# A longer pause in the preparation of w_out's sums, an earlier cast of one product's weights, and earlier last stores, in a fused attention and feed-forward kernel

## The chip, the cores and the metric

The kernel runs on one core of one Trainium2 chip. The core has a matrix engine (PE), a vector engine (DVE), a scalar engine (ACT), and queues that issue transfers; in this kernel nearly all transfers are issued by the queue SP, and some by ACT. The metric is the device time of the whole launch in microseconds, the median of the runs shown: 1046.59 us before (three runs, 1045.86 to 1046.83).

## The reference

The reference computes attention with a sigmoid in the place of softmax, puts the heads side by side, and sends the result through a feed-forward block of two products with a leaky ReLU between:

```python
# q, k, v: (8, 12, 448, 64); w_in: (768, 2048); w_out: (2048, 768)
scores = (1 / sqrt(64)) * q @ k.T - log(448)
attn = 1 / (1 + exp(-scores))
x = heads_side_by_side(attn @ v)          # (3584, 768)
h = x @ w_in
g = maximum(0.01 * h, h)
out = (g @ w_out).astype(float32)         # (3584, 768)
```

The 96 heads are worked as 48 pairs. Products keep the accuracy of float32: each operand is split into a high and a low part of a type that PE multiplies at full rate, and a product is the sum of three: high by high, high by low, low by high. "CAST" on ACT (or "COPY" on DVE) makes a high part, and a subtraction on DVE (`TENSOR_TENSOR w<-wx,w`, `lo<-x,hi` and so on) the low part.

## The kernel before

**Three stages.** In the first (0 to about 254 us of the span) 24 rounds work two head pairs each: scores (`sc`), sigmoid on ACT (`s<-sc`), and the product with v (`pv`). In the second (to about 661 us) x is multiplied with w_in in four groups of rows p, and for each group in four units u; a unit is a Strassen-like scheme of seven products n in the order 0, 1, 4, 5, 3, 6, 2, each of two halves of 18 matmuls, about 1.8 us a half. Their sums in PSUM (`px_h`, `py_h`, `pz_h`) are copied by ACT and added by DVE to four results (`c_h`), which ACT takes through the leaky ReLU; DVE forms further sums of them (`s`), and all are stored to memory (`g_n`). In the third stage 52 products of 36 matmuls each, 7.2 us, multiply sums of the stored g (a product's operand `gf` is a sum of up to three loaded tiles `g`, its parts are `gh` or a reused `g1s`, and `g`) with sums of w_out (`w_k`), in two accumulators in turn (`acc_A`, `acc_B`), from which DVE and ACT read outputs (`o`).

**The weights are prepared meanwhile.** The weights come as 64-bit numbers and are turned into float32 and summed by DVE, in work that fills gaps: the generator `prep()` (line 385) does it in small steps, first for the 8 units of w_in and then for the 8 units of w_out. A unit of w_out is read in four pieces of five conversions each (`wd<-wr`, `wd<-wd`); after the second piece 4 blocks, after the third 2 blocks are stored, and after the fourth `second()` (line 354) works through the table STEPS: sums among the eight blocks of two tiles `d` and `s`, with stores of blocks that are done (`t<-wd`, to the memory that the third stage loads as `w<-t`). In the middle, right after the store of `d` blocks 6 and 7, the table has an entry `("wait",)`; there the generator yields some steps with no work, as `rest()` (line 350) says. The fourth sum behind the pause, "s7" below, overwrites block 7 of `s`, and the store that reads `s` blocks 5 to 7 is issued after a unit's first sum; a sum that overwrites a stored block must wait until that store has landed. `d` and `s` change roles from unit to unit.

**What sets the order.** Every instruction is held in program order on its engine. `slot()` (line 169) counts `now`; `later(n, f)` puts f into the slot n ahead. A round of attention has five slots, a half product of the second stage one, a product of the third stage one. In attention `prepare(pace, time)` gives `prep()` a number of steps a slot; in the second stage `fill()` gives up to four steps a slot as long as a modelled DVE queue is short. `now` is 123 when the second stage begins. Before the change `rest()` yields 9 steps when `now` is below ALONE = 100 and 1 step afterwards.

**Last stores.** `after()` (around line 713) takes each finished result: leaky ReLU one slot later, store two or three slots later. For the last unit of the last group (`ends`) the stores go through ACT's queue, in ACT's order, the others through SP's.

**The first products of the third stage.** `work()` (line 1059) orders what stands at product k: low parts, reads of the accumulator, `whole()` and `high()` of operands up to k + 3, `high()` and `low()` of weights. `weights[WW[0]]` is `w_3`, the weights of the fourth product (k = 3): the first three are loaded and split during the second stage. `g_load(k)` (line 982) loads the operands up to k + FAR as far as tiles are spare; tiles are handed out from a list, so which tile an operand's sum gets depends on what was loaded before it. A transfer also waits for the one eight before it on the same hardware lane.

Of the kernel before, what the change touches and what calls it, by code (L numbers as in the profile page):

```python
# [26 lines left out]
AHEAD, FAR, SPARE = 5, 6, 1  # L27
GG, OO, WW = 7, 8, (3, 3)
# [2 lines left out]
PACES = 4, 5, 4.2, 2.8, 2  # L31
TIMES = 1.92, 1.92, 2.33, 2.33, 1.66
PRODUCT, LESS, MOST = 1.8, 0.2, 4
WAIT, REST = 9, 1
ALONE = 100
LATER = 4
IDLE = 7
# [60 lines left out]
def attn_ffn_kernel(ctx: ExitStack, tc: tile.TileContext, qk, v, w_in, w_out, out):  # L98
# [60 lines left out]
    def leaky(out, in_):  # L159
        act(out=out, in_=in_, func=AF.Prelu, alpha=0.01)  # L160


    now, chores = 0, {}

    def later(slots, *fns, first=False):

        chores.setdefault(now + slots, ([], []))[not first].extend(fns)

    def slot(work=None):
        nonlocal now  # L170
        for fns in chores.pop(now, ()):
            for fn in fns:
                fn()
        if work is not None:
            work()
        now += 1
# [52 lines left out]
    class Quad:  # L229
# [14 lines left out]
        def take(self, what, acc, how=copy):  # L244
            t = self.pool.tile([P, 2, S], F32, tag=self.tag, name=f"{what}_{self.name}", bufs=self.bufs)
            how(out=t, in_=acc)
            return t
# [101 lines left out]

    def rest():  # L350

        return (None for _ in range(WAIT if now < ALONE else REST))

    def second(u, k, dec):

# [28 lines left out]
    def prep():  # L384
# [22 lines left out]
        for at, (m, k) in enumerate(pieces):  # L407
# [29 lines left out]
            if k == n - 1:  # L437
                prepared.add((w, u))
                if w == 0:
                    yield from rest()  # L440
# [139 lines left out]
    class Operands:  # L580
# [30 lines left out]
        def sum(self, n, a, b):  # L611
            if n == 2 and self.s2 is None:
                self.s2 = take(f"s2_{self.p}", F32)
            to, fn, x, y = {
                3: (self.x(0), sub, self.x(0), self.x(2)),
                2: (self.s2, sub, self.x(3), self.x(0)),
                1: (self.x(2), add, self.x(2), self.x(3)),
                4: (self.x(1), sub, self.x(1), self.s2)}[n]
            fn(to[:, a:b], x[:, a:b], y[:, a:b])
            if b == NB:  # L620
                self.got.add(n)
# [62 lines left out]
    class First:  # L684
# [26 lines left out]
        def after(self, quad, c, u, n):  # L711
            got = quad.done(n)
            if got is None:
                return
            p = self.p
            row, col, t = got

            ends = p == NQ - 1 and u == NU // 2 - 1

            def save(x, t):  # L720
                (dma_act if ends else dma)(out=gd[p][x][:, 2 * u % KQ:2 * u % KQ + 2], in_=t)

            def name(row, col):
                return f"{((0, 3), (1, 2))[2 * u // KQ][col]}{row}"

            def made(x, fn, a, b):
                new = st.tile([P, 2, S], F32, tag="st", name=f"{x}_{p}_{u}", bufs=ST)
                (add if fn == "add" else sub)(new, c[a], c[b])
                c[x] = new
                later(2, lambda: save(x, new))  # L730

            c[name(row, col)] = t
            if n != 2:
                later(1, lambda: leaky(t, t))
            later(2 if n == 2 else 3, lambda: save(name(row, col), t))
            z = LATER if u == NU // 2 - 1 and p < NQ - 1 else 0
            have = set(c)
            i = 0
            for x in MADE[p % 2]:
                if x[0] not in c.planned and {x[2], x[3]} <= have | c.planned:  # L740
                    c.planned.add(x[0])
                    later(2 + i + z, lambda x=x: made(*x))
                    i += 1
# [22 lines left out]
    def go(todo, work):  # L766


        for x, what in todo:
            for y in what.split():  # L770
                later(0, lambda x=x, y=y: x.do(y))
        slot(work)
# [77 lines left out]
    total = NF * NQ // 2  # L850
    spare, homes = [(gp, f"g{n}") for n in range(GG)], {}
# [125 lines left out]
    operands = []  # L977
    for k in range(total):
        operands.append(Operand(k))
    ahead = 0  # L980

    def g_load(k):

        nonlocal ahead
        room = SPARE + sum(x.needs() for x in operands[:k + 5] if x.x is None)
        while ahead < min(k + FAR + 1, total) and len(spare) >= len(operands[ahead].new) - len(operands[ahead].raw) + room:
            operands[ahead].load()
            ahead += 1

    weights = [Wide(k, t2a) for k in range(WW[0])]  # L990
# [4 lines left out]
    ahead = READY + 2  # L995
# [27 lines left out]
    ends = max(i for i, x in enumerate(PRODUCTS) if x[2] and x[1] == PRODUCTS[-1][1])  # L1023
    outs, accs = {}, {}

    def place(p, o):
        c, pair, t = (int(x) for x in o)
        b = 4 * p + 2 * pair + t
        return out[NM * c:NM * c + NM, :, b * S:(b + 1) * S]

    def store(p, o):
        dma(out=place(p, o).rearrange("m p s -> p m s"), in_=outs.pop((p, o)))
# [8 lines left out]
    def read(k):  # L1041
        p, i = divmod(k, NF)
        for x in PRODUCTS[i][4]:
            how, o = x[0], x[1:4]
            if how == "c":
                outs[p, o] = outp.tile([P, NM, S], F32, tag="out", name=f"o{p}_{o}")
            for rows, acc in accs[PRODUCTS[i][1]][1]:
                take(how, outs[p, o][:, rows], acc)
            if x[4:]:
                later(1, lambda o=o: store(p, o))  # L1050

    g_load(-1)
    for x in weights[WW[0]:AHEAD]:
        x.load()
    for k in range(total):
        p, i = divmod(k, NF)
        _, lane, begins, _, reads = PRODUCTS[i]
        ending = k == total - 1
        def work():
            for x in operands[k:k + 3]:  # L1060
                if x.hi and not x.has_low:
                    x.low()
            if k:
                read(k - 1)
            for x in operands[k:k + 4]:
                if x.x is None:
                    x.whole()
                    x.high()
            for x in weights[WW[0]:k + 4]:
                if k and not x.has_high:  # L1070
                    x.high()
                elif x.has_high and not x.has_low and x.k < k + 3:
                    x.low()
            if begins:
                if p == NQ // 2 - 1 and i == ends:
                    three = [psum(x, f"acc_{x}{k}") for x in ("one0", "one1", lane)]
                    three[2] = three[2][:, 0]
                    accs[lane] = [x[:, :S] for x in three], [(slice(m, m + 1), x[:, None, :S]) for m, x in enumerate(three)]
                else:
                    t = psum(lane, f"acc_{lane}{k}")  # L1080
                    accs[lane] = [t[:, m, :S] for m in range(3)], [(slice(0, 3), t[:, :, :S])]
            me, w = operands[k], weights[k]
            for m in range(NM):
                todo = [(e, part, n) for e in range(KQ) for part, n in ((0, 0), (0, 1), (1, 0))]
                acc = accs[lane][0][m]
                for at, (e, part, n) in enumerate(todo):
                    mm(acc, lhsT=w.of(part, e, m), rhs=(me.hi, me.lo)[n].t[:, e],
                       start=begins and at == 0, stop=at == len(todo) - 1, skip_group_check=True)
                if ending:

                    x, = reads
                    o = x[1:4]
                    t, to = outs[p, o][:, m], place(p, o)[m]
                    for cols, queue in zip(HALVES, (dma, dma_act)):
                        take(x[0], t[:, cols], acc[:, cols])
                        queue(out=to[:, cols], in_=t[:, cols])

            me.done()
            if WW[0] <= k + AHEAD < total:
                weights[k + AHEAD].load()  # L1100
            g_load(k)

        slot(work)
# [45 lines left out]
```

## Time and profile before

| | |
|---|---|
| median of three runs | 1046.59 us (1045.86 to 1046.83) |
| the profiled execution's own time | 1049.28 us |
| its span, from the first to the last instruction | 1047.2 us |
| granted clock of TensorE, mean | 0.995 |
| PE busy | 1032.3 us, 99% of the span |
| DVE busy | 844.9 us, 81% |
| ACT busy | 583.9 us, 56% |
| DMA | 286 GB/s over the span |

The profiled execution is a fourth one, 2.69 us longer than the median of the runs. In the rows of the timeline, the first number is the start in us from the span's start, the second the time until the row's last instruction ends; then the engine, the line, the operation, the tile written and those read, the shape, and how many instructions the row holds. In brackets stands the idle time of the engine before it and what ended it. All instructions have the line of one helper (L135), so they are told apart by the tiles.

### The profile page before, as it was taken

How to read it: one execution, taken by the hardware profiler on the slowest of the kernel's cores; microseconds unless marked ns; L12 is line 12 of the kernel's file. 1: busy time of each engine (PE TensorE's matmuls, PEld its weight loads, DVE VectorE, ACT ScalarE, POOL GpSimd, SP SyncE). 2: the span in 40 equal slices, each digit the busy share in tenths (PEclk: the TensorE clock that was granted, in tenths of full speed). 3: DMA queues.
4: the chain of work that ended last, by engine and by line, in shares of the span. 5: the costliest groups of instructions: out<-in, count | busy, mean ns of one | idle time of the engine just before them, and what ended most of it. 6: DMA issues, size and time to landing. Idle time of an engine off the chain costs nothing.

```text
span 1047.2 us, 15127 instructions
## 1 busy us (share of the span) xinstructions
PE 1032.3 (99%) x5738; PEld 865.6 (83%) x5738; DVE 844.9 (81%) x992; ACT 583.9 (56%) x610; POOL 0.3 (0%) x5
## 2 busy tenths in 40 slices
PE   9999999999999999999999999989999999999998
PEld 5545555545899999999999999979999999999997
DVE  4778898788998999999855657598998888899883
ACT  6778787876554655555545555464363536444430
POOL 0000000000000000000000000000000000000000
PEclk9999999999999999999999999989999999999999
DMA  7888787889889898899876878996668798766823
GB/s 274 295 281 283 268 279 257 299 292 314 272 300 356 280 346 302 315 350 376 315 238 207 302 281 319 377 360 267 255 244 306 268 402 312 270 226 247 322 94 131
DMA packets 113847, 300.62 MB, mean 287 GB/s; under 512 B 9712, under 2 KB 51824, under 8 KB 113776
## 3 DMA queue, kind: packets, MB, share of 16 engines
q1 hardware_dynamic: 111760, 295.20, 79.2%
q10 hardware_dynamic: 2016, 4.47, 1.2%
q8 instruction: 45, 0.74, 0.3%
q14 instruction: 26, 0.21, 0.1%
HBM read 202.77 MB, written 96.86 MB: 286 GB/s over the span
## 4 chain that ended last, share of the span: by engine, by line
PE 94%; DVE 3%; DMA 1%; issue 0%; ACT 0%; ACTq 0%; DVEq 0%
PE px_h L135 21%; PE acc_A L135 18%; PE acc_B L135 18%; PE pz_h L135 11%; PE pv L135 11%; PE sc L135 10%; PE py_h L135 5%; DVE wd L135 2%; DMA t<-wd 1%; PE acc_one L135 0%; DVE w L135 0%; DVE lo L135 0%; DVE qks L135 0%; DVE x L135 0%; DVE gf L135 0%
## 5 line engine op out<-in xcount | busy, mean ns | idle before, releaser
L135 PE MATMUL px_h<-hi,w 128*128 128x448 f32 x768 | 223.6, 362 | 2.0 <-DVE w L135 2.0
L135 PEld LDWEIGHTS px_h<-hi,w 128*128 128x128 f32 x768 | 143.8, 187 | 11.9 <-DVE w L135 2.4
L135 PE MATMUL acc_A<-gh,w 128*128 128x448 f32 x528 | 152.5, 363 | 0.0
L135 DVE TENSOR_TENSOR w<-wx,w 128x768 fp32r<-128x768 f32 x112 | 106.8, 953 | 48.8 <-ACT w L135 48.8
L135 PE MATMUL px_h<-lo,w 128*128 128x448 f32 x384 | 139.2, 362 | 0.0
L135 ACT ACTIVATE s<-sc 128x896 f32<-128x896 f32 x144 | 119.7, 934 | 11.7 <-PE sc L135 11.7
L135 PE MATMUL acc_B<-gh,w 128*128 128x448 f32 x416 | 122.6, 369 | 3.1 <-ACT o L135 2.0
L135 PE MATMUL pz_h<-hi,w 128*128 128x448 f32 x384 | 113.0, 362 | 1.2 <-DVE w L135 1.2
L135 PE MATMUL pv<-s,v 128*64 128x448 f32 x576 | 113.8, 544 | 0.0
L135 PEld LDWEIGHTS acc_A<-gh,w 128*128 128x128 f32 x528 | 99.1, 188 | 6.5
L135 PEld LDWEIGHTS sc<-qks 64*128 64x128 f32 x876 | 80.9, 189 | 25.7 <-issue 16.9
L135 PE MATMUL sc<-qks 64*128 64x448 f32 (+1 forms) x876 | 96.5, 371 | 2.4 <-DVE x L135 2.2
L135 ACT CAST w<-wx 128x768 fp32r<-128x768 f32 x112 | 91.3, 832 | 4.4 <-DMA wx<-t 4.4
L135 PEld LDWEIGHTS pv<-s,v 128*64 128x64 f32 x576 | 39.1, 137 | 64.0 <-issue 54.1
L135 ACT ACTIVATE c_h<-c_h 128x896 f32<-128x896 f32 x48 | 45.8, 954 | 82.2 <-DVE c_h L135 82.2
L135 DVE TENSOR_TENSOR w<-w 128x1536 fp32r<-128x1536 f32 x52 | 90.9, 1750 | 0.0
L135 PEld LDWEIGHTS acc_B<-gh,w 128*128 128x128 f32 x416 | 79.6, 192 | 9.2 <-ACT o L135 2.4
L135 PE MATMUL acc_B<-g,w 128*128 128x448 f32 x328 | 85.6, 365 | 0.0
L135 PEld LDWEIGHTS pz_h<-hi,w 128*128 128x128 f32 x384 | 71.9, 187 | 5.9 <-DVE w L135 1.5
L135 PEld LDWEIGHTS px_h<-lo,w 128*128 128x128 f32 x384 | 72.1, 188 | 5.6
L135 ACT CAST w<-w 128x1536 fp32r<-128x1536 f32 x52 | 76.6, 1476 | 0.1
L135 DVE SCALAR_TENSOR_TENSOR wd<-wr,wd 128x384 int32<-128x384 int32 x128 | 71.3, 557 | 3.4
(97 smaller groups left out, 1585.0 us busy)
## 6 DMA issues: line engine op xcount, KB each, us to landing
wx<-t SPq DMA_DIRECT2D x112, 384.0 KB, 4.8
w<-t SPq DMA_DIRECT2D x52, 768.0 KB, 4.3
g<-g SPq DMA_DIRECT2D x34, 896.0 KB, 7.0
g<-c_h SPq DMA_DIRECT2D x60, 448.0 KB, 4.5
g<-s SPq DMA_DIRECT2D x48, 448.0 KB, 5.5
qk<-in_qk SPq DMA_DIRECT2D x46, 448.0 KB, 5.3
g1s<-g SPq DMA_DIRECT2D x18, 896.0 KB, 6.6
wr<-in_w_in SPq DMA_DIRECT2D x32, 384.0 KB, 4.7
```

What stands on the lines that cost most here:

```text
L135: return lambda *args, **kw: tc.keep_in_program_order(issue(*args, **kw))
```

## The change

Four things change. First, `rest()` yields 9 steps as long as `now` is below FFN = 126, that is to the end of attention, and 3 instead of 1 afterwards. Second, the last unit's stores on ACT's queue are put one slot behind the result instead of two or three. Third, `g_load(0)` loads one operand less than before. Fourth, at k = 1 the cast of `w_3` is put ahead of operand 4's sum and cast, and its low part ahead of operand 4's low part.

```diff
-WAIT, REST = 9, 1
+WAIT, REST = 9, 3
+FFN = 126
 ALONE = 100
@@ def rest():
-        return (None for _ in range(WAIT if now < ALONE else REST))
+        return (None for _ in range(WAIT if now < FFN else REST))
@@ after()
             if n != 2:
                 later(1, lambda: leaky(t, t))
-            later(2 if n == 2 else 3, lambda: save(name(row, col), t))
+            later(1 if ends else 2 if n == 2 else 3, lambda: save(name(row, col), t))
@@ g_load(k)
-        while ahead < min(k + FAR + 1, total) and len(spare) >= len(operands[ahead].new) - len(operands[ahead].raw) + room:
+        while ahead < min(k + FAR + 1 - (k == 0), total) and len(spare) >= len(operands[ahead].new) - len(operands[ahead].raw) + room:
             operands[ahead].load()
             ahead += 1
@@ work()
             if k:
                 read(k - 1)
+            if k == 1:
+                weights[WW[0]].high()
             for x in operands[k:k + 4]:
                 if x.x is None:
                     x.whole()
                     x.high()
             for x in weights[WW[0]:k + 4]:
                 if k and not x.has_high:
                     x.high()
-                elif x.has_high and not x.has_low and x.k < k + 3:
+                elif x.has_high and not x.has_low and (x.k < k + 3 or k == 1):
                     x.low()
```

The number of instructions on each engine stays as it was, and PE's order too. On DVE the order near the end of attention (the sums of w_out's second unit, and the last rounds' splits `qks` and copies `x`) was:

```order
L135 TENSOR_TENSOR wd_1_2190<-wd_1_2190 128x192
L135 SCALAR_TENSOR_TENSOR wd_1_2190<-wd_1_2190 128x384
L135 TENSOR_TENSOR qks_2646<-qk_2496,qks_2646 128x832
L135 TENSOR_TENSOR wd_1_2190<-wd_1_2190 128x192
L135 TENSOR_TENSOR wd_0_2189<-wd_1_2190 128x192
L135 TENSOR_TENSOR wd_1_2190<-wd_1_2190 128x192
L135 TENSOR_TENSOR qks_2664<-qk_2557,qks_2664 128x832
L135 SCALAR_TENSOR_TENSOR wd_1_2190<-wd_0_2189,wd_1_2190 128x192
L135 TENSOR_TENSOR wd_0_2189<-wd_1_2190 128x192
L135 COPY x_2690<-pv_2648 128x448
```

and now it is:

```order
L136 SCALAR_TENSOR_TENSOR wd_1_2190<-wd_1_2190 128x192
L136 TENSOR_TENSOR qks_2646<-qk_2496,qks_2646 128x832
L136 TENSOR_TENSOR qks_2662<-qk_2557,qks_2662 128x832
L136 COPY x_2683<-pv_2648 128x448
L136 TENSOR_TENSOR wd_1_2190<-wd_1_2190 128x192
L136 SCALAR_TENSOR_TENSOR wd_1_2190<-wd_1_2190 128x384
L136 TENSOR_TENSOR wd_1_2190<-wd_1_2190 128x192
L136 TENSOR_TENSOR wd_0_2189<-wd_1_2190 128x192
L136 TENSOR_TENSOR wd_1_2190<-wd_1_2190 128x192
L136 SCALAR_TENSOR_TENSOR wd_1_2190<-wd_0_2189,wd_1_2190 128x192
```

The sum s7 of this unit, `wd_0_2189<-wd_1_2190 128x192` (the first row of that form), stood ahead of a `qks` and of the `COPY x`; now both `qks` and the `COPY x` stand ahead of it.

On DVE at the first products of the second stage (the low parts of its weights, `w_0_n`, beside the sums of w_out's third unit) the order was:

```order
L135 TENSOR_TENSOR wd_0_2189<-wd_0_2189 128x192
L135 TENSOR_TENSOR wd_1_2190<-wd_0_2189 128x192
L135 TENSOR_TENSOR wd_0_2189<-wd_0_2189 128x192
L135 SCALAR_TENSOR_TENSOR wd_0_2189<-wd_1_2190,wd_0_2189 128x192
L135 TENSOR_TENSOR w_0_0_2896<-wx_0_2728,w_0_0_2896 128x2x384
L135 TENSOR_TENSOR wd_1_2190<-wd_0_2189 128x192
L135 TENSOR_SCALAR wd_1_2190<-wr_3_0_2776 128x384
L135 TENSOR_TENSOR w_0_1_2910<-wx_1_2782,w_0_1_2910 128x2x384
```

and now it is:

```order
L136 TENSOR_TENSOR wd_0_2189<-wd_0_2189 128x192
L136 TENSOR_TENSOR w_0_0_2884<-wx_0_2718,w_0_0_2884 128x2x384
L136 SCALAR_TENSOR_TENSOR wd_0_2189<-wd_0_2189 128x192
L136 TENSOR_TENSOR w_0_1_2902<-wx_1_2769,w_0_1_2902 128x2x384
L136 COPY x_2801<-pv_2870 128x448
L136 TENSOR_TENSOR lo_0_2941<-x_654,hi_0_2929 128x1344
L136 TENSOR_TENSOR w_0_4_2943<-wx_4_2797,w_0_4_2943 128x2x384
L136 TENSOR_TENSOR wd_0_2189<-wd_0_2189 128x192
L136 SCALAR_TENSOR_TENSOR wd_0_2189<-wd_0_2189 128x384
L136 TENSOR_TENSOR wd_0_2189<-wd_0_2189 128x192
L136 TENSOR_TENSOR wd_1_2190<-wd_0_2189 128x192
```

The first weights' low parts stood behind the unit's s7 (`wd_1_2190<-wd_0_2189 128x192`, the first of the two rows of that form); now three of them stand ahead of it, the first with four of the unit's sums between.

On ACT at the fourth product of the third stage (casts of operand 4, of `w_3` and of `w_4`, and the copy of the accumulator `acc_B` that frees it) the order was:

```order
L135 COPY o_111_6476<-acc_A_6429 128x1344
L135 CAST g1s_4_6417<-gf_6478 128x1792
L135 CAST w_3_6421<-w_3_6421 128x1536
L135 CAST w_4_6423<-w_4_6423 128x1536
L135 COPY o_101_6526<-acc_B_6484 128x1344
```

and now it is:

```order
L136 COPY o_111_6474<-acc_A_6429 128x1344
L136 CAST w_3_6421<-w_3_6421 128x1536
L136 CAST g1s_4_6417<-gf_6477 128x1792
L136 CAST w_4_6423<-w_4_6423 128x1536
L136 COPY o_101_6527<-acc_B_6483 128x1344
```

The cast of `w_3` stands ahead of operand 4's; the copy of `acc_B` still stands behind all three. On DVE the low part of `w_3` moves likewise from behind operand 5's sum to a place right behind operand 4's sum. That sum, `gf<-g_4,g_4`, lies in another tile than before: the old one also held sums `s` of the second stage, and the sum waited for four transfers, stores of `s` among them; in the new one it waits for the two loads of its own operands.

## The prediction

> **What bounds the kernel now.** I read the page's first part, then the waits of PE, then the timelines of DVE, ACT and PE around each wait, then the transfers behind them. The first part has PE at work nearly all the time, and the waits of PE (total us, times, longest us) are few:
>
> ```profile
> PE 1032.3 (99%) x5738; PEld 865.6 (83%) x5738; DVE 844.9 (81%) x992; ACT 583.9 (56%) x610; POOL 0.3 (0%) x5
> ...
> PE sc L135 <- DVE x L135: 2.2, 1, 2.2
> PE acc_B L135 <- ACT o L135: 2.0, 1, 2.0
> PE px_h L135 <- DVE w L135: 2.0, 1, 2.0
> PE pz_h L135 <- DVE w L135: 1.2, 1, 1.2
> PE acc_B L135 <- DVE w L135: 1.1, 1, 1.1
> ```
>
> So PE bounds the kernel, and an edit of other engines' order can win only these five waits and what hangs on them. They lie at two places.
>
> **The end of attention.** DVE's timeline there:
>
> ```profile
> 233.41 0.75 DVE L135 TENSOR_TENSOR wd<-wd 128x192 f32<-128x192 f32 x2 [3.65 <-DMA t<-wd]
> ...
> 254.76 0.75 DVE L135 TENSOR_TENSOR wd<-wd 128x192 f32<-128x192 f32 x2 [3.48 <-DMA t<-wd]
> ...
> 255.70 0.95 DVE L135 TENSOR_TENSOR w<-wx,w 128x768 fp32r<-128x768 f32 x1
> ...
> 266.46 1.55 DVE L135 TENSOR_TENSOR lo<-x,hi 128x1344 fp32r<-128x1344 f32 x1
> ```
>
> Twice DVE, which works in order, stands for 3.5 us before s7, because s7 overwrites a block whose store is still under way. Behind the first stall stands the `COPY x` that empties PSUM for the next scores (PE's wait `sc <- DVE x`), behind the second the low part of the first weights (255.70, `px_h <- DVE w`), and in its wake, behind the `lo` at 266.46, that of the fourth product (`pz_h <- DVE w`). PE's timeline shows what each costs:
>
> ```profile
> 231.90 2.09 PE L135 MATMUL sc<-qks 64*128 64x448 f32 x18
> ...
> 238.26 4.73 PE L135 MATMUL pv<-s,v 128*64 128x448 f32 x24
> ...
> 244.59 3.91 PE L135 MATMUL sc<-qks 64*128 64x448 f32 x36
> ...
> 254.00 0.48 PE L135 MATMUL px_h<-hi,w 128*128 128x448 f32 x1
> ...
> 260.02 0.36 PE L135 MATMUL py_h<-hi,w 128*128 128x448 f32 x1
> ...
> 267.22 0.36 PE L135 MATMUL pz_h<-hi,w 128*128 128x448 f32 x1
> ...
> 272.25 0.36 PE L135 MATMUL px_h<-hi,w 128*128 128x448 f32 x1
> ```
>
> The stalled round's 36 score matmuls take 238.26 - 231.90 = 6.36 us, the next round's 3.91: 2.45 lost. Two undisturbed products take 267.22 - 260.02 = 7.20, so 3.60 each; the first takes 260.02 - 254.00 = 6.02 (2.42 lost), the fourth 272.25 - 267.22 = 5.03 (1.43 lost). Together **6.30 us**.
>
> **The fourth product of the third stage.** First ACT, DVE and PE, then clock and transfers by stretch (length; busy PE, PEld, DVE, ACT, POOL; granted clock, DMA share, GB/s), and the load of `w_3` by itself (KB, us to landing), which is issued at 668.48:
>
> ```profile
> 679.20 1.70 ACT L135 CAST g1s<-gf 128x1792 fp32r<-128x1792 f32 x1 [3.90 <-DVE gf L135]
> 680.79 2.85 ACT L135 CAST w<-w 128x1536 fp32r<-128x1536 f32 x2
> 683.54 1.27 ACT L135 COPY o<-acc_B 128x1344 f32<-128x1344 f32 x1
> ...
> 675.08 2.03 DVE L135 TENSOR_TENSOR gf<-g,g 128x1792 f32<-128x1792 f32 x1 [2.05 <-DMA g<-s]
> ...
> 684.81 3.42 DVE L135 TENSOR_TENSOR w<-w 128x1536 fp32r<-128x1536 f32 x2
> ...
> 675.45 0.37 PE L135 MATMUL acc_A<-gh,w 128*128 128x448 f32 x1
> ...
> 684.87 0.47 PE L135 MATMUL acc_B<-gh,w 128*128 128x448 f32 x1 [2.05 <-ACT o L135]
> 686.61 1.11 PE L135 MATMUL acc_B<-gh,w 128*128 128x448 f32 x2 [1.07 <-DVE w L135]
> ...
> 696.29 0.36 PE L135 MATMUL acc_A<-g1s,w 128*128 128x448 f32 x1
> ...
> 656.00:660.00 4.00, 4.00 (x22) 3.75 (x21) 2.24 (x3) 1.90 (x2) 0.00 (x0) 1.00 0.92 319
> 660.00:670.00 10.00, 10.00 (x52) 9.38 (x51) 4.87 (x5) 3.58 (x3) 0.00 (x0) 1.00 0.99 362
> ...
> 686.00:692.00 6.00, 5.39 (x14) 4.79 (x15) 6.00 (x5) 1.98 (x2) 0.00 (x0) 0.50 1.02 417
> ...
> 668.48 3.45 SPq L135 DMA_DIRECT2D w<-t  x3
> w<-t SPq DMA_DIRECT2D x1, 768.0 KB, 10.4
> ```
>
> Operand 4's sum `gf` waits 2.05 us for a store of `s`; ACT, in order, waits 3.90 for that sum, and so the two casts and the `COPY o` behind it, which frees `acc_B`, are late; then PE waits for the low part of `w_3`; then the clock is at 0.50. Two products of 36 matmuls at 0.2 us are 14.4; they take 696.29 - 675.45 = 20.84. That is **6.44 us** lost: 684.87 less the undisturbed 682.66 gives 2.21 for the first wait, some 1.3 for the second (1.74 from 684.87 to 686.61 less two matmuls), and the rest, about 3.0, for the half clock.
>
> The sum of both is **12.7 us**; no edit here can win more than that, since PE's instructions stay the same.
>
> **Part 1, nine steps of pause, near 230.** Both `qks` and the `COPY x` now stand ahead of s7. The copy needs only PE's `pv`, done when the scores start at 231.90; I put it at 233, and PE wants the bank half a round later, at 231.90 + 1.95 = 233.85. s7 comes after the copy and three more short sums (the row at 233.41 holds two in 0.75), so at about 234.5; the store landed at 233.4, where DVE's stall ended. No wait is left: 2.45 won. Were the store later than that, s7 would hold up conversions only, not the copy.
>
> **Part 1, the first products, near 252.** Of the 3.85 us won or lost with 255.70, all hangs on when DVE reaches that low part. The rows for it:
>
> ```profile
> 238.34 0.35 DVE L135 TENSOR_SCALAR wd<-wr 128x384 int32<-128x384 int32 x1
> ...
> 240.58 0.35 DVE L135 TENSOR_SCALAR wd<-wr 128x384 int32<-128x384 int32 x1
> ...
> 245.50 0.62 DVE L135 COPY x<-pv 128x448 f32<-128x448 f32 x1
> ...
> 247.21 0.76 DVE L135 TENSOR_TENSOR wd<-wd 128x576 f32<-128x576 f32 x1
> ...
> 249.40 0.36 DVE L135 TENSOR_TENSOR wd<-wd 128x192 f32<-128x192 f32 x1
> ```
>
> The `COPY x` at 245.50 follows PE and comes 2.45 earlier, at 243.05. In the new order one more conversion row and two pieces of 240.58 - 238.34 = 2.24 us stand behind it, so the unit's sums begin at about 243.05 + 0.54 + 0.55 + 4.48 = 248.6. The low part of `w_0_0` stands behind the sum that ends 249.76 - 247.21 = 2.55 after that start, at about 251.1, and is done at 252.0. PE begins the first product at 254.00 - 2.45 = 251.55, and needs it after two and a half matmul times, at about 252.1. This is a tie. I bound its cost by 0 and 2.0 (the wait it has now), and take 0.2, since an error of the sum above in a row or two is 0.3 to 0.6. The next low parts stand a copy, a `lo` and a few sums behind and have a whole product of 3.6 us each; the one that was late for the fourth product now stands behind no conversions, only behind a `c_h` and a `lo`, and comes ahead of need by about half a us, an estimate. s7 of this unit has two low parts (0.9 each), a copy (0.55), a `lo` (1.5) and four short sums (0.4) between it and 252.0, so it comes near 257.4. Its store is issued behind the unit's first sum and landed 254.76 - 247.97 = 6.8 us after that sum's end; now 248.6 + 0.76 + 6.8 = 256.2, some 1 us sooner. Won here: 6.30 - 0.2 = **6.1**, with bounds 3.9 and 6.3 for the place.
>
> **Part 1, the second stage.** The work pushed back is done there later. DVE and PE by stretch:
>
> ```profile
> 272.00:400.00 128.00, 128.00 (x642) 119.99 (x641) 118.70 (x172) 70.59 (x81) 0.00 (x0) 1.00 0.90 315
> ```
>
> PE has no gap although DVE is 93% busy, so the cost is nothing as long as what is pushed back only fills DVE's gaps later on. If that cover went, see the last rival.
>
> **Part 2, the earlier last stores.** One store on ACT's queue comes two slots of 1.8 us earlier. What it can delay is the last weights of the second stage:
>
> ```profile
> 654.09 0.83 ACT L135 CAST w<-wx 128x768 fp32r<-128x768 f32 x1 [1.20 <-DMA wx<-t]
> ...
> 655.83 1.08 DVE L135 TENSOR_TENSOR c_h<-c_h,px_h 128x896 f32<-128x896 f32 x1
> ...
> 657.45 0.36 PE L135 MATMUL px_h<-hi,w 128*128 128x448 f32 x1
> ```
>
> The cast waits for its load; the `c_h` sum behind the low part ends at 656.91, and PE needs the bank at 657.45. A delay of up to 0.54 is hidden. The store moves 448 KB, about 1.1 us at the 417 GB/s of the full stretch from 686 on, so the cost is 0 to 0.5; I take 0.1. [...]
>
> **Parts 3 and 4, the fourth product.** `gf` no longer waits for the stores and can start when DVE is free, 675.08 - 2.05 = 673.03, so it is done at 677.1 instead of 679.2. But ACT now takes `w_3` first, and `w_3` lands at 668.48 + 10.4 = 678.9. Behind it stand 1.38 (cast of `w_3`), 1.59 (operand 4), 1.38 (`w_4`) and 1.27 (`COPY o`), from the pitches of the rows above: 684.5, and PE 0.06 later, 684.6, against 682.66: **1.94 us still lost**, if `w_3` lands when it does now. It should land somewhat earlier, since the store and the loads behind it start earlier: in 656 to 670 the transfers fell 4 x (1 - 319/417) + 10 x (1 - 362/417) = 2.3 us short of the full rate. So 0 to 2.3 sooner; I take 0.7, a third of it, because one store and one load move and the rest of the queue is bound by its own waits. Lost then: 1.25. The low part of `w_3` follows its cast at once and ends near 682, ahead of PE; the second wait goes. DVE then runs without a gap: 680.3 + 1.7 + 1.94 + 1.94 + 1.7 + 1.94 + 1.5 = 691.0 for the read of `acc_A` that the fifth product needs at 684.6 + 7.2 = 691.8; both move with the landing. 0 to 0.3, I take 0.1.
>
> The clock decides 3.0 us. In the rows it fell after 2.05 and 1.07 of idle with two matmuls between, while one wait of 2.24 near 234 (page's waits: 2.2) and one of 2.0 near 255 were followed by full-length rows (244.59: 36 in 3.91). One idle of 1.25 should not drop it. [...] The row at 686 differs: it has half clock with PE never idle longer than 2.05, so the measurement makes the price possible. Won here: 6.44 - 1.25 - 0.1 = **5.1**, with bounds 1.2 (1.94, a half clock of 3.0 and 0.3 remain) and 6.4 (it lands 1.94 sooner).
>
> **The sum.** 6.1 + 5.1 - 0.1 = 11.1 us. The profiled execution, 1049.28 with a span of 1047.2, would become about 1038.2 and 1036.1; it is 2.69 above the median of the runs, to which I apply the same gain: 1046.59 - 11.1 = **1035.5 us**.
>
> **Rivals.** (a) The cast of `w_3` only swaps one late thing for another: it lands as now, PE idles 1.94, and the clock falls as before. For it: the 10.4 us of that load and a DMA share of 1.02. Against: one idle in place of two. Price 0.7 + 3.0: 1039.2. (b) The tie at 252 is lost, or s7 at 257 still meets its store, and `c_h` and `w_0_5` behind it are late. For it: 1 us of margin against a landing of 6.8. Price 2 to 4: about 1038.5. (c) The change does not do what it says: DVE reaches the same sums under the same stores, and the waits only change their names. Against it the new order, in which both `qks`, the copy and three low parts pass s7. 1045 to 1047. (d) Slower: five units of w_out are summed in the second stage, later than before, and there the pause is 3 steps. If s7 stood less than 6.8 us behind its store in each, DVE could stop 3.65 us five times, 18 us, under full load at 93%, with PE behind: 1046.6 - 11 + 18 = 1053.6. Against it: DVE interleaves the products' own work, more than a dozen instructions between store and s7, which at 118.70/172 = 0.69 us are over 9 us. It decides from where these fall below 6.8.
>
> **Chances.** Forecast 0.65, (a) 0.15, (b) 0.13, (c) 0.03, (d) 0.04. The forecast's own range is 1034 to 1037.5; with (a) and (b) 1033.7 to 1040.7. Less than 0.2% (2.1 us) cannot be told from no change; faster by more: 0.65 + 0.15 + 0.13 + 0.01 = 0.94, within 0.02, slower 0.04.
>
> **What would show it.** Right: no `DVE wd <- DMA t<-wd` and no `PE sc <- DVE x` among the waits; 3.9 for the scores near 232; 3.6 for the first and the fourth product of the second stage, or up to 4 for the first; one wait `PE acc_B <- ACT o` of 1 to 2 us near 683, with the ACT queue headed by a cast of `w` that waits for `w<-t`; clock 1.00 around 686. Wrong: a DMA wait of DVE between 255 and 540, a wait of PE before `px_h` near 657, or a stretch at 0.50 behind the third stage's start.

## The result, and the profile after

The changed kernel takes 1035.61 us, the median of four runs (1034.58 to 1037.74), against 1046.22 (1044.91 to 1046.83) for the kernel before on the same chip: a ratio of 0.9903, 95% interval 0.9882 to 0.9924. It is faster by 10.6 us; forecast was 11.1. Its profiled execution takes 1034.62, with a span of 1032.8.

PE's waits in that profile are one, at the very start, before anything was loaded; of the five waits shown before none is left, and no DVE wait on `t<-wd`:

```profile
PE 1026.5 (99%) x5738; PEld 862.5 (84%) x5738; DVE 845.2 (82%) x992; ACT 584.1 (57%) x610; POOL 0.3 (0%) x5
...
PE unread L136 <- DVE zeros L752: 1.0, 1, 1.0
```

The spans of the two profiles differ by 1047.2 - 1032.8 = 14.4, more than the 12.74 that the change could win at all. The rest is the start, where the two kernels have the same instructions in the same order. PE by shape in the first 12 us (count, busy us, mean ns of one), of before and then of after:

```profile
L135 PE MATMUL sc<-qks 64*128 64x224 f32 x24 | 3.0, 434 | 0.2 <-ACT qks L135 0.2
...
L135 PE MATMUL sc<-qk 64*64 64x448 f32 x8 | 1.8, 977 | 0.0
```

```profile
L136 PE MATMUL sc<-qks 64*128 64x224 f32 x24 | 2.0, 322 | 0.1
L136 PE MATMUL sc<-qk 64*64 64x448 f32 x8 | 1.6, 558 | 0.0
```

The first score matmuls ran slowly in the one execution and fast in the other, and the first `pv` starts at 9.86 against 8.12: 1.74 us in which the instructions are the same in both kernels. It is the clock: a trace's records of a full clock begin at 9.93 us in this profile of before and at 4.80 in that of after, where a single score matmul takes 0.41 us at 4.35 and 0.27 at 4.86 (rows by stretch show a clock of 1.00 also where there is no record yet). Further profiles show both: the first `pv` starts at 7.8 to 8.3 in ten of all fourteen, with records from 3.8 to 5.9 on, and at 9.8 to 10.3 in four, with records from 9.7 to 10.2 on. So the time of one execution is uncertain by some 1.7 us from there alone. Of the four, two are the only two profiles of the kernel before; whether that is chance, and how much of the difference of the medians it makes, no run shows. Set against this, the profiles say: 1.74 at the start, 6.23 at the end of attention, 6.44 at the fourth product, 14.41 in all.

**The end of attention**, DVE and then PE of the changed kernel:

```profile
230.91 0.62 DVE L136 COPY x<-pv 128x448 f32<-128x448 f32 x1 [2.23 <-ACT x L136]
...
232.31 1.01 DVE L136 TENSOR_TENSOR wd<-wd 128x192 f32<-128x192 f32 x3
...
246.69 0.76 DVE L136 TENSOR_TENSOR wd<-wd 128x576 f32<-128x576 f32 x1
...
249.16 0.95 DVE L136 TENSOR_TENSOR w<-wx,w 128x768 fp32r<-128x768 f32 x1
...
254.90 1.01 DVE L136 TENSOR_TENSOR wd<-wd 128x192 f32<-128x192 f32 x3
...
230.15 3.91 PE L136 MATMUL sc<-qks 64*128 64x448 f32 x36
233.99 4.73 PE L136 MATMUL pv<-s,v 128*64 128x448 f32 x24
...
249.73 0.48 PE L136 MATMUL px_h<-hi,w 128*128 128x448 f32 x1
...
253.48 0.36 PE L136 MATMUL py_h<-hi,w 128*128 128x448 f32 x1
...
260.68 0.36 PE L136 MATMUL pz_h<-hi,w 128*128 128x448 f32 x1
...
264.28 0.36 PE L136 MATMUL px_h<-hi,w 128*128 128x448 f32 x1
```

The stalled round runs in 3.91, the first product takes 253.48 - 249.73 = 3.75, the fourth 264.28 - 260.68 = 3.60. The two rows with x3 hold s7 of the second and of the third unit; neither waits. The low part of the first weights ends at 250.11, and PE's third matmul starts at 250.25 without a wait: the tie of the prediction was won by 0.14 us. The first product still takes 0.15 longer than the fourth, without a wait.

**The fourth product**, ACT, DVE and PE, and the clock by stretch (columns as in the prediction):

```profile
668.67 1.48 ACT L136 CAST w<-w 128x1536 fp32r<-128x1536 f32 x1 [3.95 <-DMA w<-t]
670.05 1.69 ACT L136 CAST g1s<-gf 128x1792 fp32r<-128x1792 f32 x1
671.65 1.47 ACT L136 CAST w<-w 128x1536 fp32r<-128x1536 f32 x1
673.03 1.27 ACT L136 COPY o<-acc_B 128x1344 f32<-128x1344 f32 x1
...
663.49 2.02 DVE L136 TENSOR_TENSOR gf<-g,g 128x1792 f32<-128x1792 f32 x1
...
674.68 0.36 PE L136 MATMUL acc_B<-gh,w 128*128 128x448 f32 x1
...
674.68:681.88 7.20, 7.20 (x38) 6.75 (x37) 7.10 (x5) 3.08 (x2) 0.00 (x0) 1.00 1.02 422
```

`gf` does not wait, ACT heads its queue with the cast of `w_3` and waits 3.95 for its load, and `COPY o` ends at 674.30, 0.38 ahead of PE. The product takes 7.20 at full clock.

### The profile page after: what moved, and what is told of

Read it like the earlier page. It is cut to its first block, busy times and chain, and to the rows that moved or that the text cites. A ratio compares the mean times of both kernels' runs of the same rounds, so it can differ in the third digit from the quotient of the medians.

```text
span 1032.8 us, 15121 instructions
## 1 busy us (share of the span) xinstructions
PE 1026.5 (99%) x5738; PEld 862.5 (84%) x5738; DVE 845.2 (82%) x992; ACT 584.1 (57%) x610; POOL 0.3 (0%) x5
## 4 chain that ended last, share of the span: by engine, by line
PE 99%; ACT 0%; ACTq 0%; DVE 0%; DVEq 0%; issue 0%
PE px_h L136 22%; PE acc_A L136 18%; PE acc_B L136 18%; PE pv L136 13%; PE sc L136 11%; PE pz_h L136 11%; PE py_h L136 6%; PE acc_one L136 0%; ACTq L136 0%; ACT L136 0%; DVE o L136 0%; ACT qks L136 0%; DVEq L1148 0%; ACT warm L136 0%
## 5 line engine op out<-in xcount | busy, mean ns | idle before, releaser
L136 PEld LDWEIGHTS px_h<-hi,w 128*128 128x128 f32 x768 | 144.1, 188 | 10.3 <-issue 0.7
L136 PE MATMUL acc_B<-gh,w 128*128 128x448 f32 x416 | 120.3, 363 | 0.0
```

Of the source, the lines that this page charges most:

```text
L136: return lambda *args, **kw: tc.keep_in_program_order(issue(*args, **kw))
```

## The experiments

The two first profiles and those of the twelve runs make one table. Times of `w_3`'s landing and of the sum `gf` count from the first matmul of the third stage; "lost" is what the third and the fourth product of the third stage take over 14.40 together (from the start of `acc_A` at k = 2 to that at k = 4). The runs were taken in four sets, in which the kernel before took 1046.22, 1045.17, 1045.39 and 1045.48 us; ratios and gains below are against the kernel before of the same set, and a row with one run has only that one.

| kernel | median us (runs) | PE's waits in attention's end | `gf` starts | `w_3` lands | lost at k = 3 |
|---|---|---|---|---|---|
| before | 1046.22 (4) | 2.2, 2.0, 1.2 | 14.03 | 17.84 | 6.44 |
| before, again | 1046.36 (12) | 1.9, 1.6, 1.2 | 14.18 | 17.78 | 5.15 |
| pause alone | 1036.73 (6) | none | 12.55 | 17.14 | 3.77 |
| all but the pause | 1040.50 (6) | 2.0, 1.3, 1.2 | 10.05 | 14.74 | 0.11 |
| the change | 1035.61 (4) | none | 10.41 | 15.57 | 0.00 |
| the change, again | 1034.88 (5) | none | 10.89 | 16.42 | 0.65 |
| late stores | 1035.68 (6) | none | 10.91 | 15.51 | 0.00 |
| old tile | 1035.96 (6) | none | 11.26 | 14.87 | 0.00 |
| late cast | 1035.05 (6) | none | 11.33 | 17.22 | 0.96 |
| pause of one step later on | 1036.70 (6) | none | 11.12 | 17.33 | 1.54 |
| `w_3` loaded first | 1034.51 (5) | none | 11.11 | 1.73 | 0.00 |
| `w_3` loaded last | 1038.66 (1) | none | 10.19 | 18.31 | 3.97 |
| three casts of `w_4` | 1041.43 (1) | none | 11.21 | 17.32 | 7.10 |
| four casts of `w_4` | 1041.97 (1) | none | 10.88 | 16.81 | 7.12 |

**The change once more.** No edit.

> The changed kernel once more, beside the others of this set. Its first profile has no wait of PE at the end of attention nor at the fourth w_out product, and a clock of 1.00, while its runs spread from 1034.6 to 1037.7 us. If that spread comes from the start (30 first score matmuls in 2.65 us there, in 4.17 us in the profile before), this profile differs from the first only in the first 10 us, by up to 1.7 us, or not at all. Rival: the spread comes from the place of the tie near 250 us or from the landing of w_3 near 668 us; then a wait of PE of 0.3 to 2 us shows there.

Measured 1034.88 us (1034.39 to 1038.00), ratio to before 0.9905 (0.9884 to 0.9926). This profile has the quick start too; it shows a wait at the fourth product, with `w_3` 0.85 later than in the first profile. So the landing of `w_3` differs from execution to execution, as the start does. Which of them made the run of 1038.0 stays open, since that run has no profile; its mean granted clock of 0.999 speaks against a window at half clock, which would take about 0.0016 off by itself (half of 3.41 us in 1036).

**The pause alone.**

```diff
 # the kernel before, with
-WAIT, REST = 9, 1
+WAIT, REST = 9, 3
+FFN = 126
-        return (None for _ in range(WAIT if now < ALONE else REST))
+        return (None for _ in range(WAIT if now < FFN else REST))
```

> The kernel before with the pause alone (9 steps to the end of attention, 3 after). Theory: it wins the whole loss at the end of attention, 6.3 us (2.45 + 2.42 + 1.43), so 1046.2 - 6.3 = 1039.9 us; its profile has no DVE wait on t<-wd, and keeps the waits acc_B <- ACT o of 2.0 and acc_B <- DVE w of 1.1 with a clock of 0.5 behind them. Rival: the stall of the third unit only moves to the first products; then about 2.5 to 4 us are won, 1042 to 1044.

Measured 1036.73 us (1034.76 to 1040.29), ratio 0.9914 (0.9894 to 0.9934): 8.4 us won, 2.1 more than expected. The end of attention went as the theory says: no wait, and 6.11 us of it gone between the profiles. What was not expected stands at the fourth product. PE's waits there, and `gf` on DVE:

```profile
PE acc_B L136 <- DVE w L136: 1.1, 1, 1.1
...
PE acc_B L136 <- ACT o L136: 0.6, 1, 0.6
...
667.46 2.03 DVE L136 TENSOR_TENSOR gf<-g,g 128x1792 f32<-128x1792 f32 x1 [1.85 <-DMA g1s<-g]
```

The loss is 3.77 instead of 6.44, though nothing was edited there. `gf` starts 1.5 us sooner after the third stage's start than in the kernel before (the row names a load; the store on which it waits was issued at 656.98 and took 10.3, to 667.26). Its tile is handed out with the pause at another place of the ring that the sums `s` use: it waits for the store of the second of the last four sums, landed 12.37 us after the third stage's start, instead of that of the third, landed at 13.81 in the kernel before. So the pause wins something at a second place too (how much is rough: before, again lost 5.15 there and not 6.44), and the parts do not add up: 8.4 and 4.7 (the next experiment) are 13.1, together they win 10.3 on the same chip.

**All but the pause.**

```diff
 # the changed kernel, with
-WAIT, REST = 9, 3
+WAIT, REST = 9, 1
-        return (None for _ in range(WAIT if now < FFN else REST))
+        return (None for _ in range(WAIT if now < ALONE else REST))
```

> The changed kernel with the old pause (9 steps only in the first part of attention, 1 after). Theory: it wins at the fourth w_out product alone, 5.1 to 6.4 us, so 1039.8 to 1041.1 us, and keeps the waits sc <- DVE x of 2.2, px_h <- DVE w of 2.0 and pz_h <- DVE w of 1.2. Rival: the two places are coupled (the transfers' load after the second stage hangs on when the preparation ends), and w_3 lands later here; then a wait acc_B <- ACT o of 1 to 2 us shows, 1041 to 1045.

Measured 1040.50 us (1039.59 to 1041.46), ratio 0.9953 (0.9936 to 0.9971), 4.7 won. The profile has the three waits at the end of attention and next to nothing at the fourth product:

```profile
PE sc L136 <- DVE x L136: 2.0, 1, 2.0
PE px_h L136 <- DVE w L136: 1.3, 1, 1.3
PE pz_h L136 <- DVE w L136: 1.2, 1, 1.2
```

So it is the pause that mends the end of attention; against the changed kernel this profile loses 5.20 us there (2.23 + 1.51 + 1.46). The rival of a coupling in this direction did not show: in this profile `w_3` lands at 14.74, sooner than anywhere else with that order of loads.

**Late stores.** The prediction said that the earlier last stores let `w_3` land sooner.

```diff
-            later(1 if ends else 2 if n == 2 else 3, lambda: save(name(row, col), t))
+            later(2 if n == 2 else 3, lambda: save(name(row, col), t))
```

> The changed kernel with the last unit's stores at two and three slots as before. Theory (the prediction's: the earlier stores are what lets w_3 land sooner): w_3 lands about 2.3 us later against PE than in the changed kernel, COPY o is late by as much less its margin of 0.4, and PE waits 1.9 us before acc_B: 1.9 us slower than the changed kernel, with a clock of 1.0, or 4.9 slower if the clock falls. Rival (w_3 lands sooner because of the other edits, the order of loads on SP above all): no difference within 0.5 us.

Measured 1035.68 us (1034.32 to 1040.39), ratio 0.9915 (0.9892 to 0.9938). The cast of `w_3`, which starts when the load is there, starts at the same time as in the changed kernel, 668.67:

```profile
668.66 1.47 ACT L136 CAST w<-w 128x1536 fp32r<-128x1536 f32 x1 [3.41 <-DMA w<-t]
```

The 2.3 us later that the expectation named did not come, so nothing supports my reason. One profile cannot exclude a smaller effect, since the landing differs by 0.85 between the two profiles of the changed kernel itself. Two of the six runs, 1038.29 and 1040.39, are longer than any of the changed kernel; they have no profile, and the medians cannot be told apart.

**Old tile and late cast.** One part undone each.

```diff
 # old tile
-        while ahead < min(k + FAR + 1 - (k == 0), total) and ...
+        while ahead < min(k + FAR + 1, total) and ...
 # late cast
-            if k == 1:
-                weights[WW[0]].high()
-                elif x.has_high and not x.has_low and (x.k < k + 3 or k == 1):
+                elif x.has_high and not x.has_low and x.k < k + 3:
```

> The changed kernel with g_load(0) as before, so that operand 4's sum lies in the tile of the sums s again and waits for one of their stores. Theory of the prediction: the sum starts later (the store lands 12 to 15 us after the third stage's start, the sum starts at 10.4 without it), ACT's cast of operand 4 then comes after w_3's; with the store at 12.2 the sum ends at 16.3 and w_3's cast at 17.0, so nothing is lost; with the store at 15.2 the sum ends at 19.3, COPY o ends 2.3 later than in the changed kernel and PE waits 1.9 us. Here the tile is that of the second store of s, by the waits of its program, so: no difference within 0.5 us. Rival (the tile is what mends the fourth product): 2 to 5 us slower.

> The changed kernel with the cast and the low part of w_3 at their old places, behind operand 4's and operand 5's sums. Theory: gf ends 14.5 us after the third stage's start, operand 4's cast 16.2, the two casts of w 17.6 and 19.8 with w_3 landing at 15.6, COPY o 21.1: no wait for it (21.6); DVE comes to the low part of w_3 at 20.2 and ends it at 21.9, PE needs it at 22.0: 0 to 0.5 us slower. Rival (the early cast is what mends the fourth product): waits acc_B <- DVE w of 1 us or more and a clock of 0.5 behind, 2 to 4 us slower.

Old tile: 1035.96 us (1034.80 to 1039.02), ratio 0.9911 (0.9892 to 0.9930); late cast: 1035.05 us (1034.24 to 1035.81), ratio 0.9900 (0.9883 to 0.9917). Neither can be told from the whole change. Old tile lost nothing in its profile, in which `gf` waited 1.2 us for a store and was done long before the cast of `w_3`; but `w_3` landed at 14.87 there, so a late landing was not tried with it. With the late cast PE waits 0.3 us:

```profile
PE acc_B L136 <- DVE w L136: 0.3, 1, 0.3
```

Two pairs with `w_3` landing alike (17.1 to 17.3) say more. Pause alone and late cast both cast `w_3` late; in late cast the other tile brings `gf` 1.2 sooner, and 3.77 becomes 0.96 (the earlier stores differ too). Late cast and the next kernel both have the other tile; the early cast does not better 0.96, it makes 1.54 (the pause in the second stage differs too). These are single profiles, so the sizes are rough. But the early cast has no gain to show: when the load is late, ACT's whole queue stands behind it. Since undoing any one of the last three parts leaves the time where it was, the runs do not say which of them the fourth product needs; what they show is that the pause alone leaves a loss of 3.77 there, and that all three without the pause leave 0.11.

**A pause of one step in the second stage.** This tests the slower rival of the prediction.

```diff
-WAIT, REST = 9, 3
+WAIT, REST = 9, 1
```

> The changed kernel with a pause of 1 step in the second stage instead of 3. Theory: s7 stands more than 9 us behind its store there in either case, so there is no DVE wait on t<-wd between 270 and 540 us and no difference: within 0.5 us. Rival (the prediction's slower case, the store meets s7 in the second stage): waits DVE wd <- DMA t<-wd of up to 3.6 us for each of five units, hidden by DVE's gaps or not: 0 to 18 us slower.

Measured 1036.70 us (1034.88 to 1038.40), ratio 0.9917 (0.9899 to 0.9935): no difference that can be told from the changed kernel's 0.9905. DVE has no wait on `t<-wd` from 270 to 545 us here either, so the slower rival is not near with one step. The profiled execution, 1038.40, has the slower start (1.70) and the longest wait seen at the fourth product with this order, by the term that the prediction had written down, `COPY o` 5.6 us behind the landing of `w_3`:

```profile
PE acc_B L136 <- ACT o L136: 1.3, 1, 1.3
...
672.40 1.48 ACT L136 CAST w<-w 128x1536 fp32r<-128x1536 f32 x1 [5.02 <-DMA w<-t]
...
676.75 1.27 ACT L136 COPY o<-acc_B 128x1344 f32<-128x1344 f32 x1
```

`COPY o` ends at 678.02, 5.62 after the cast began, and PE is late by what is missing.

**The kernel before once more.** No edit.

> The kernel before once more, with its own profile. In its first profile the first scores ran slowly to about 8 us (1.7 us that are no part of the change), and the fourth product lost 6.44 us. If the loss at the fourth product is a fixed part of that kernel, this profile shows it again at 6.4; if it hangs on how full the transfers are in that execution (the rival: with the pause alone the same place lost 3.8 us in the profile of that run, and its fastest run cannot have lost anything there), it is between 1 and 6.4 and the wait before gf differs. The end of attention must show 6.3 in either case.

Measured 1046.36 us (1041.03 to 1047.48, twelve runs). Against the changed kernel's profile the end of attention lost 5.43 here (2.18 + 1.79 + 1.46; 6.23 in the first profile), the fourth product 5.15. So neither loss is a constant: the first varies with the landing of the stores (DVE waits for `t<-wd` for 6.2 us in all here and for 7.1 in the first profile), the second mainly with the clock (one window at half clock here, two in the first profile; a window is 3.41 us, since each stretch at half clock between the first and the last products is recorded as 3.41 or 6.83 us long). The runs of the kernel before spread over 6.5 us, those of the changed one over 3.6.

**`w_3` loaded first, and last.** If the landing of `w_3` and what stands behind its cast set the wait, moving the load must move it.

```diff
 # first: load ahead of the last operands' loads; w_4's cast behind COPY o
+    weights[WW[0]].load()
     g_load(-1)
-    for x in weights[WW[0]:AHEAD]:
+    for x in weights[WW[0] + 1:AHEAD]:
         x.load()
-            if k == 1:
-                weights[WW[0]].high()
+            if k in (1, 2):
+                weights[WW[0] + k - 1].high()
-            for x in weights[WW[0]:k + 4]:
+            for x in weights[WW[0]:k + 4 - (k == 1)]:
 # last
-    for x in weights[WW[0]:AHEAD]:
+    for x in weights[WW[0]:AHEAD][::-1]:
```

> The changed kernel with the load of w_3 put ahead of operand 4's and 5's last loads on SP, and the cast of w_4 behind COPY o on ACT. In the profiles so far with the early cast COPY o ends 5.65 us after w_3 lands, and PE needs it 21.6 us after the third stage's start; w_3 landed 14.7 to 17.8 after it, so the wait was 0 to 1.4. Theory (the landing of w_3 and what stands behind its cast set this wait): w_3 lands before 13 here, COPY o ends before 20 whatever the transfers do, PE never waits, and the slow runs of the changed kernel but for the start's 1.7 us go: 1034.5 to 1036.5 us. Rival (the wait hangs on the transfers' load as a whole, and operand 4's sum or w_4 becomes late in w_3's place): a wait before acc_A or acc_B of 0.5 us or more.

> The changed kernel with the load of w_3 behind that of w_4 on SP (ACT's order unchanged). Theory: w_3 lands where w_4 did, 17.4 to 19.4 us after the third stage's start, COPY o 5.65 later, 23.0 to 25.0, so one wait acc_B <- ACT o of 1.4 to 3.4 us against 0 to 1.4. On the clock: in the profiles so far it fell for a window of 3.41 us when the window before it had PE idle for 1.64 us or more of its 3.41 (48%), and not when it had 1.30 or less (38%), windows counted on from the recorded fall. By that it falls here if 1.64 or more of the wait lies in one window. [...]

First: 1034.51 us (1034.43 to 1035.35), ratio 0.9897 (0.9877 to 0.9917). The cast of `w_3` no longer waits for its load, and `COPY o` is done 2.2 us ahead of PE, at 672.03 against 674.27:

```profile
663.83 1.50 ACT L136 CAST w<-w 128x1536 fp32r<-128x1536 f32 x1
669.16 1.70 ACT L136 CAST g1s<-gf 128x1792 fp32r<-128x1792 f32 x1 [3.83 <-DVE gf L136]
670.76 1.27 ACT L136 COPY o<-acc_B 128x1344 f32<-128x1344 f32 x1
```

Its five runs lie within 0.92 us, and none is above 1035.4; by the intervals it cannot be called faster than the change, and as the cast of `w_4` was moved too, the load's share is not shown apart. Last: the wait is 2.2, as the theory has it for a landing at 18.31 (18.31 + 5.65 - 21.60 = 2.36), and the clock falls:

```profile
PE acc_B L136 <- ACT o L136: 2.2, 1, 2.2
...
673.48:676.89 3.41, 1.44 (x8) 1.00 (x6) 3.41 (x3) 3.41 (x3) 0.00 (x0) 1.00 1.02 429
676.89:680.30 3.41, 3.14 (x8) 2.81 (x9) 3.41 (x2) 1.86 (x3) 0.00 (x0) 0.50 1.03 429
680.30:683.70 3.40, 3.40 (x18) 3.18 (x17) 3.32 (x2) 1.44 (x2) 0.00 (x0) 1.00 1.00 407
```

One single wait was enough for it here, and cost 3.97 instead of 2.4.

**The clock by itself.** `w_4` is cast three and four times, which only delays `COPY o`.

```diff
                 if k and not x.has_high:
                     x.high()
+                    for _ in range(2 if k == 1 else 0):     # 3 in the other
+                        x.high()
```

> The changed kernel with the cast of w_4 done three times instead of once, so that COPY o comes 2.76 us later. Theory: one wait acc_B <- ACT o of 2.76 - 0.4 = 2.4 us where w_3 lands at 15.6, up to 4.2 where it lands at 17.3. [...]

> As the one with three casts of w_4, with four: COPY o 4.14 us later, one wait of 3.8 us (up to 5.5). [...]

The waits were 4.3 and 5.3 us (loads at 17.32 and 16.81), and the clock fell in both. In the one with four casts, by stretches that begin where the clock's records do:

```profile
673.59:677.00 3.41, 1.49 (x8) 1.05 (x6) 3.41 (x2) 3.35 (x3) 0.00 (x0) 1.00 1.03 430
677.00:680.41 3.41, 0.06 (x1) 0.06 (x1) 1.56 (x2) 3.38 (x4) 0.00 (x0) 1.00 1.01 419
680.41:683.82 3.41, 3.41 (x9) 3.05 (x10) 2.40 (x2) 2.84 (x2) 0.00 (x0) 0.50 1.01 420
```

Here the window that PE spent 1.92 us idle was not followed by a fall, the next one, idle but for 0.06, was. With `w_3` last a window with 1.97 idle was followed by one, and with the pause alone one with 1.64:

```profile
675.77:679.18 3.41, 1.77 (x8) 0.99 (x7) 3.41 (x3) 3.32 (x4) 0.00 (x0) 1.00 1.02 425
679.18:682.60 3.42, 3.42 (x10) 3.02 (x10) 3.42 (x3) 1.18 (x1) 0.00 (x0) 0.50 1.01 418
```

So what the expectation for `w_3` last worked out from the profiles, a fall behind 1.64 us idle or more, does not hold in every window. What stays: the clock fell here without a wholly idle window (with `w_3` last the only gap is 2.25 us long), and idle of 1.6 to 2 us in one window was followed by a fall twice (1.64, 1.97) and once not (1.92).

## Why the prediction was right

**The end of attention: right in place, mechanism and size.** Forecast 6.1 won, measured 6.23 between the profiles. The working holds in detail once 1.74 us of the start are taken off: the unit's sums were to begin at 248.6 - 1.74 = 246.9 and begin at 246.69, the low part of `w_0_0` was to be done at 250.3 and is at 250.11, s7 was to come at 255.7 and the row that holds it starts at 254.90. Of the 0.2 us for the tie 0.15 came, in the first product, but without the wait that they stood for. The rival that the first products stay late, and that s7 meets its store, did not show in any of eleven profiles with the pause.

**The second stage and the slower rival: right.** No DVE wait on `t<-wd` between 270 and 545 us, even with a pause of one step. Taken by its words, one sign of being wrong, a DMA wait of DVE between 255 and 540, did come: a wait of 0.7 us of a sum `s` for `g<-c_h`. It is no store of the preparation, and PE does not wait there.

**The earlier last stores: cost 0.1 forecast, none found, and the use that I gave them not borne out.** PE has no wait before `px_h` in either order: its only wait is the 1.0 us at the start, in the first profile of the changed kernel as in that with late stores.

**The fourth product: right in mechanism, mis-sized in one term.** That `COPY o` ends 5.6 us behind `w_3`'s landing is exact (5.63 in the first profile, 674.30 - 668.67). The term that was off is the landing: "0 to 2.3 sooner; I take 0.7, a third of it". It was 17.84 - 15.57 = 2.27 sooner in the first profile and 1.42 in the second, so 1.25 us lost became 0.00 and 0.65. The sign that I had named, one wait of 1 to 2 us near 683, did not come in the first profile and was 0.4 in the second. And the reason given for an earlier landing has no support: with late stores it is 15.51. In ten profiles with that order of loads and all or part of the change `w_3` lands anywhere from 14.7 to 17.3; in the kernel before at 17.8 both times. Much of that spread is there already when its load is issued. In five of the ten, SP issues it 4.3 to 4.8 us after the third stage's start, and it lands by 16.4; in the other five SP issues it at 5.0 to 6.7, and it lands at 16.8 or later. The load itself takes 10.5 to 12.1 us in all ten. In each, the load ahead of it in SP's queue had waited for a store (`g<-c_h`). In the first profiles of before and after `w_3`'s load waited for such a store itself, 0.9 and 0.8 us, and was issued 0.36 us after it had landed (at 668.12 and 657.33): the 607 transfers of each of these profiles share eight semaphores, and none is issued before the one ahead of it on the same semaphore has landed. What makes these stores land early or late in an execution stays open.

**The clock: right for the change, with too kind an argument.** It did not fall between the first and the last products in either profile of the changed kernel, whose waits there were 0.0 and 0.4, and all nine of its runs have a mean granted clock of 0.999 or 1.0; of the twelve runs of the kernel before, ten have 0.995 to 0.998. But "one idle of 1.25 should not drop it" rested on waits of 2.24 and 2.0 in attention that left it alone, and with `w_3` last one idle of 2.25 did drop it. Windows of 3.41 us counted back from the recorded fall, an estimate, suggest why: the wait near 234 was cut by a window's end into 1.22 and 1.02, that near 255 into 1.0 and 1.0. Rival (a), a stall of 1.94 with a fall, was nearer than 0.15 says: in the one run in which `w_3` landed at 18.3, it came about.

**The sum.** 11.1 forecast, 10.6 measured between the medians (8.0 to 12.3 by the interval). The first two profiles, less the start, say 12.7, the two taken again 5.46 + 4.50 = 10.0. The sum was worked out from one execution, and its loss at the fourth product differs by 1.3 us from one execution to the next; so that it came within 0.5 us of the medians is in part luck, while the places and the waits are not.

## What to carry to other kernels

When an in-order engine waits for a store that reads a block it is to overwrite, look at who is queued behind it: a pause that lets the work of others pass won 6 us here, at no cost that the runs show. A cast put first in a queue showed no gain here, and where its load is late, the whole queue waits behind it; with the load moved ahead (and one cast moved back) no wait was left in the one profile of it. And a loss that hangs on the landing of a transfer has a spread, so read it from several profiles before giving it a size.

## What the runs showed of the hardware that I had not expected

- The first score matmuls take 434 ns in one execution and 322 in another of the same instructions, and the first `pv` starts at 8.1 or 9.8 to 10.3 us: 1.7 to 2.2 us in the time of a launch that no edit made. The records of a full clock begin accordingly, at 3.8 to 5.9 or at 9.7 to 10.2 us.
- The clock fell to half behind windows of 3.41 us in which PE had been idle 1.64 us (pause alone), 1.97 (`w_3` last), 2.28 (before), 2.74 (before, again), 2.96 (three casts) and 3.35 (four casts), and not behind one of 1.92 (four casts). What else decides stays open. With `w_3` last the one window at half clock cost 3.97 - 2.41 = 1.6 us.
- A pause far ahead changed which tile of a ring an operand got 400 us later, and with it the store that it waits for: 1.5 us sooner, with no edit near it.
